# Attention units of 384, 384 and 320 columns, and one token order for all batches, in a polysketch attention and mixture-of-experts kernel

## The chip, the cores and the metric

The kernel runs on one core of a Trainium2 chip. A core has five engines that run their own instruction queues and meet only through semaphores: PE (TensorE, matrix products), DVE (VectorE), ACT (ScalarE), POOL (GpSimd) and SP, which in this kernel issues nearly all DMAs. The metric is the device time of one launch in microseconds; lower is better. The time given is the median of several runs; the profile is one profiled execution.

## The reference, cut to what matters

There are 4 batches, 4 heads, 1088 tokens and head dimension 32; then 4352 tokens of width 128 go through 4 experts with hidden width 1024. Everything is float32.

```
def phi(x):                       # polynomial sketch, 8 x 8 = 64 features
    a = einsum('rd,bhsd->bhsr', S1, x); b = einsum('rd,bhsd->bhsr', S2, x)
    return einsum('bhsi,bhsj->bhsij', a, b).reshape(..., 64)
q_p, k_p = phi(q), phi(k)
kv  = einsum('bhsf,bhsd->bhfd', k_p, v);   z = sum(k_p, axis=s)
x   = (q_p @ kv) / (q_p @ z + 1e-6)        # then (B,H,S,D) -> (B*S, H*D)
p   = domain_probs / (sum(domain_probs) + 1e-9)
out = sum over e of p[:, e] * (relu(x @ w1[e]) @ w2[e])
```

The attention of a batch needs all its keys first (kv and z sum over tokens). After that each token's query row is independent, and so is each token in the experts.

## The kernel before, in words

**Columns.** Tokens are columns of the tile `xT` (128 features x 4352). Inside a batch, column c stands for token (c % 32) * 34 + c // 32 (G = 34): a partition of the loaded `qn` holds 34 consecutive tokens, and a 32x32 vector transpose turns 32 partitions into 32 neighbouring columns. The last batch is the exception in this kernel: its columns are loaded as 30 tokens per partition for the first 960 columns and 4 per partition for the last 128 (lines 95 to 97), so that its last 128 columns are 128 tokens in a row. The loads of the gate probabilities `dp` and `ends` (lines 150 to 158) and the output addresses (lines 860 and 904) follow that order.

**Expert work: chunks and steps.** `CHUNKS` cuts the 4352 columns into 11 chunks (128, 448, six of 512, 320, 256, 128), and `START` gives their first columns: 0, 128, 576, 1088, 1600, 2112, 2624, 3136, 3648, 3968, 4224. A chunk takes 16 steps: 4 experts times 4 pairs of hidden blocks. In a step, `first` makes two halves: each is a product `h` into one of three PSUM banks (pool `ps_h`), a relu on ACT (line 817), and one or two rectify-and-subtract instructions on DVE (line 786) that make the operand combinations for a 7-product scheme. After `first(i)` comes `second(i - 2)`: seven products `o` of half the chunk's width. Products use half the array's columns (64) each; `on_side` hands them to the two halves in turn. After the fourth step of an expert, `gather` copies `o` on ACT and POOL adds the pieces and multiplies by the gate (lines 923 to 943). Chunks 0 and 10 are plain (no 7-product scheme).

**Attention work: pieces.** The attention of batches 1 to 3 and of the rest of batch 0 is a generator, `front`. It is cut into pieces by its `yield`s: 19 pieces for the keys of a batch (three transposes `key_turn`, line 328; three projections on PE; eight products `key_product` on DVE, line 391, whose both inputs are in SBUF; `key_sum` on PE) and 20 pieces for each unit of query columns (transpose, projection, three shuffles, four products `qp` (line 501), then `attend`: PE products, reciprocal, multiplication, a transpose to `y` (line 591), four stores to the DRAM tile `xd` (line 609) and one load into `xT` (line 617)). `UNITS` gives the widths of a batch's units. A unit of up to three 128-column blocks uses one bank in `attend`, a wider one uses two.

**What sets the order.** The queues are written out by this Python program. In each half step, after the relu and the rectify instructions, `work()` adds credit, and for each whole credit it emits the next piece. The credit per step is `rate`, the largest need over all later chunks:

```
rate = CHUNKS[m] / NQ * max([0] + [(needed[c] + (8 if c > 1 else 4) - done[0]) / (START[c] - gone) for c in range(m + 1, NC)])
```

`needed[c]` is the number of pieces after which the columns of chunk c are there; it follows from `UNITS` and `CHUNKS`. The rest of SP's queue (next batch's loads after its predecessor's keys, the gate loads at the sixth step of a chunk, the output stores) is placed by the same program.

Of the kernel before, what the change touches and what calls it, by code (L numbers as in the profile page):

```python
# [16 lines left out]
def _ap(t, p0: int, np_: int, off: int, free):  # L17

    p = list(t.ap)[0]
    return bass.AP(t.tensor, t.offset + p0 * p[0] + off, [[p[0], np_]] + [list(d) for d in free])  # L20
# [3 lines left out]
def kernel(  # L24
# [20 lines left out]

    nc = tc.nc

    P = 128
    HP = 64
    B, H, S, D = q.shape
    E, DM, F = w1.shape
    R = 8
    R2 = 2 * R
    G = S // 32
# [5 lines left out]
    CW = 512  # L63
    GE = 160
    LA = 2
    UNITS = [[P, 448, 512], [512, 320, 256], [448, 512, P], [384, 320, 384]]

    CHUNKS = [P, 448, 512] + [512] * 5 + [320, 256, P]
    NC = len(CHUNKS)
    START = [sum(CHUNKS[:m]) for m in range(NC)]  # L70
    assert all(sum(u) == S for u in UNITS) and sum(CHUNKS) == B * S

# [11 lines left out]
    def psum(pool, tag):  # L84
        return pool.tile([P, 512], F32, tag=tag, name=tag)


    def load_rows(src, b, name, part=slice(0, S)):

        d = kn if name == "kn" else qn  # L90
        if b not in d:
            d[b] = lpool.tile([P, S], F32, tag=name, bufs=2, name=name)
        c, n = part.start, part.stop - part.start
        base = src.offset + b * H * S * D
        if name == "qn" and b == B - 1:
            for c, n, t in ((0, (G - 4) * D, 0), ((G - 4) * D, 4 * D, S - P)):
                nc.sync.dma_start(d[b][:, c : c + n], bass.AP(src.tensor, base + t * D, [[S * D, H], [n, 32], [1, n]]))
        else:
            nc.sync.dma_start(d[b][:, part], bass.AP(src.tensor, base + c, [[G * D, P], [1, n]]))

    def load_v(b):
        t = lpool.tile([P, H * NT * D], F32, tag="vn", name="vn")
# [13 lines left out]
    kn, qn, vn = {}, {}, {}  # L116

    def load_batch(b):
        load_rows(k, b, "kn")
        vn[b] = load_v(b)  # L120
        load_rows(q, b, "qn")
# [7 lines left out]
    def load_w1(e):  # L129
        nc.sync.dma_start(w1_sb[:, e, :], w1[e])  # L130

    def load_w2(e):
        nc.sync.dma_start(w2_sb[:, e], w2[e].rearrange("(f p) d -> p f d", p=P))

    load_rows(k, 0, "kn")
    load_rows(q, 0, "qn", slice(0, P))
    vn[0] = load_v(0)
# [6 lines left out]
    dp = cpool.tile([P, G, E], F32, name="dp")  # L144

    ends = cpool.tile([P, 2, E], F32, name="ends")
    e_sum = cpool.tile([P, 2, 3], F32, name="e_sum")
    load_rows(q, 0, "qn", slice(P, S))
    load_w1(0)
    for p0, n, g0, m, t in ((0, 96, 0, G, 0), (96, 32, 0, G - 4, 3 * S), (96, 32, G - 4, 4, B * S - P)):  # L150
        nc.sync.dma_start(
            _ap(dp, p0, n, g0 * E, [[1, m * E]]),
            bass.AP(domain_probs.tensor, domain_probs.offset + t * E, [[m * E, n], [1, m * E]]),
        )
    for i, t, g in ((0, 0, G), (1, B * S - P, 4)):
        nc.sync.dma_start(
            ends[:, i, :], bass.AP(domain_probs.tensor, domain_probs.offset + t * E, [[g * E, 32], [1, 4 * E]])
        )
    load_w2(0)
    for e in range(1, E):  # L160
# [37 lines left out]
    def on_side(out, weights, moving, **flags):  # L198

        s = turn[0]  # L200
        turn[0] = 1 - s
        nc.tensor.matmul(out(s), weights(s), moving(s), **flags)  # L202
# [97 lines left out]
    def parts(m):  # L300

        c, end, at = START[m], START[m] + CHUNKS[m], 0
        while c < end:
            n = min(end, (c // S + 1) * S) - c
            yield c // S, c % S, n, at
            c, at = c + n, at + n
# [367 lines left out]
    def start():  # L674


        b, n = 0, UNITS[0][0]
        kf = []
# [39 lines left out]

        n1 = UNITS[b][1]
        qT = apool.tile([P, QW], F32, tag="qT2", name="qT2")  # L720
# [14 lines left out]
    def front():  # L735
        for b in range(B):
# [4 lines left out]
            c = 0  # L741
            for n in UNITS[b]:
                if b or c:
# [5 lines left out]
    hid, acc, total = {}, {}, {}  # L749
    NP = FB // 2  # L750

    def plain(m):
        return m in (0, NC - 1)
# [77 lines left out]
    def second(i):  # L831
        m, kq = steps[i]
        n, (e, f) = CHUNKS[m], divmod(kq, NP)
        hd = hid.pop(i)
        if plain(m):

            if f == 0:
                acc[m] = psum(ps_o, f"o{e % 2}")
            for j in range(2):
                for _ in range(2):  # L840
                    on_side(
                        lambda s: acc[m][half[s], 0:DM],
                        lambda s: hd[:, n * j + HP * s : n * j + HP * s + HP],
                        lambda s: w2_sb[:, e, 2 * f + j, :],
                        start=(f == j == 0),
                        stop=(f == NP - 1 and j == 1),
                    )
            if f == NP - 1:
                p_e = ends[:, 1 if m else 0, e : e + 1]
                if e == 0:  # L850
                    total[m] = mpool.tile([P, P], F32, tag="end", name="end")
                    nc.vector.tensor_scalar(
                        out=total[m][:, :], in0=acc[m][:, 0:DM], scalar1=p_e, scalar2=None, op0=ALU.mult
                    )
                else:
                    nc.vector.scalar_tensor_tensor(  # L856
                        out=total[m][:, :], in0=acc[m][:, 0:DM], scalar=p_e, in1=total[m][:, :], op0=ALU.mult, op1=ALU.add
                    )
                if e == E - 1:
                    t, to = (B * S - P, [[DM, P], [1, DM]]) if m else (0, [[G * DM, 32], [1, 4 * DM]])  # L860
                    nc.sync.dma_start(bass.AP(out.tensor, out.offset + t * DM, to), total.pop(m)[:, :])
            return
        if f == 0:
            acc[m, e] = [psum(ps_o, "o0"), psum(ps_o, "o1")]
            begun[:] = [0, 0]
        w = n // 2
        blk = lambda a, j: w2_sb[:, e, 2 * f + j, HP * a : HP * a + HP]
        new = lambda a: w2s[:, e, f, a, :]
        place = lambda a: hd[:, w * a : w * a + w]

        todo = (
            [(blk(0, 0), place(0)), (new(3), place(3)), (blk(0, 1), place(2)), (new(1), place(6))],
            [(new(2), place(5)), (new(0), place(4)), (blk(1, 1), place(7)), (new(1), place(6))],
        )
        at = [0, 0]
        for _ in range(7):
            s = turn[0]
            p = at[s]
            at[s] += 1

            fresh = p >= begun[s]
            begun[s] = max(begun[s], p + 1)
            wt, mv = todo[s][p]
            on_side(
                lambda s: acc[m, e][p // 2][half[s], w * (p % 2) : w * (p % 2) + w],
                lambda s: wt,
                lambda s: mv,
                start=(fresh and p % 2 == 0),
                stop=(f == NP - 1),
                skip_group_check=True,  # L890
            )

    def turn_back(m, src):

        n = CHUNKS[m]
        ob = mpool.tile([P, CW], F32, tag="ob", name="ob")
        nc.vector.transpose(ob[:, 0:n], src)
        for b, c, nn, at in parts(m):
            for a in range(4):
                nc.sync.dma_start(  # L900
                    bass.AP(
                        out.tensor,
                        out.offset + (b * S + c // 32) * DM + 32 * a,
                        [[(G - 4 if b == B - 1 else G) * DM, 32], [DM, nn // 32], [1, 32]],
                    ),
                    _ap(ob, 32 * a, 32, at, [[32, nn // 32], [1, 32]]),
                )
# [54 lines left out]

    needed, columns, count = [0] * NC, UNITS[0][0], 0
    for b in range(B):
        count += 19 if b else 0
        for n in UNITS[b] if b else UNITS[0][1:]:
            count, columns = count + (20 if count else 18), columns + n
# [8 lines left out]
    for i in range(len(steps) + LA):  # L976
        if i < len(steps):
            m, kq = steps[i]
# [34 lines left out]
        if i >= LA:  # L1013
            second(i - LA)
            mm, kk = steps[i - LA]
            if kk % NP == NP - 1 and not plain(mm):
                ending = chain(ending, gather(mm, kk // NP))
            else:
                next(ending, None)
# [29 lines left out]
```

## Time and profile before

| What | Value |
|---|---|
| median of 3 runs | 487.64 us (487.64 to 488.46) |
| the profiled execution: its own time | 487.64 us |
| its span | 485.9 us |
| PE busy | 481.5 us (99%) |
| DVE busy | 320.9 us (66%) |
| ACT busy | 246.8 us (51%) |
| POOL busy | 230.0 us (47%) |
| granted TensorE clock | 1.0 in all slices |
| DMA, q1 | 25.53 MB, 18.9% of 16 engines' span |

Busy PE time counts a product from its modelled start to its end, and products overlap, so 99% says that PE was rarely without a product. The 40 slices of the page show where an engine was busy; the list of waits says for whom an engine stood idle; the chain follows back from the last instruction to whatever released each step.

### The profile page before, as it was taken

Reading aid. Unit: us, or ns where it says so; the run is one execution under the profiler, and the core shown is the slowest. Engines: PE = TensorE matmul, PEld = TensorE weight load, DVE = VectorE, ACT = ScalarE, POOL = GpSimd, SP = SyncE. Lnnn points to the kernel's source line nnn. Section 1 sums busy time; section 2 is a strip of 40 time slices with the busy share of each in tenths; the row PEclk is TensorE's granted clock in tenths of the full one; section 3 lists DMA queues with packets and bytes.
Section 4 is the critical chain, followed back from the end, with each engine's and each line's share of the span. In section 5 each row is a group of like instructions: output and inputs, shape, how many; then the busy total and the mean of one; then the engine's idle time right before and its main releaser. Section 6 shows DMA issues by size and latency. Waiting matters only on the chain.

```text
span 485.9 us, 11377 instructions
## 1 busy us (share of the span) xinstructions
PE 481.5 (99%) x4551; PEld 362.7 (75%) x4551; DVE 320.9 (66%) x759; ACT 246.8 (51%) x496; POOL 230.0 (47%) x270
## 2 busy tenths in 40 slices
PE   8999999999999999999999999999999999999997
PEld 6965666667777777777777777677777777999997
DVE  6859675686766668486776757668684666665642
ACT  4354564445544555355445555445455555566651
POOL 5172654435444455415455444424555445555571
PEclk9999999999999999999999999999999999999999
DMA  7990050211003123031103100021101200120001
GB/s 223 278 299 10 23 150 12 88 20 45 2 9 106 24 69 93 2 89 20 40 1 130 24 12 1 3 86 24 34 0 56 50 1 0 45 55 4 15 1 20
DMA packets 37772, 26.25 MB, mean 54 GB/s; under 512 B 24824, under 2 KB 34520, under 8 KB 37208
## 3 DMA queue, kind: packets, MB, share of 16 engines
q1 hardware_dynamic: 37704, 25.53, 18.9%
q8 instruction: 36, 0.59, 0.5%
q14 instruction: 16, 0.13, 0.1%
q10 hardware_dynamic: 16, 0.00, 0.0%
HBM read 21.28 MB, written 4.24 MB: 53 GB/s over the span
## 4 chain that ended last, share of the span: by engine, by line
PE 97%; DMA 1%; DVE 1%; issue 0%; SPq 0%; ACT 0%; ACTq 0%
PE h L202 50%; PE o L202 41%; PE f L202 3%; PE den L202 2%; DMA kn<-in_k_dram 1%; PE num L202 1%; DVE qp L501 0%; DVE kp L391 0%; DVE kT L328 0%; DVE qT L488 0%; SPq L125 0%; DVE end L856 0%; DVE kvz L414 0%; ACT fs L360 0%; ACT vx L337 0%
## 5 line engine op out<-in xcount | busy, mean ns | idle before, releaser
L202 PE MATMUL h<-xT,w_sb 128*64 128x512 f32 (+5 forms) x1424 | 300.2, 491 | 0.0
L786 DVE SCALAR_TENSOR_TENSOR hid<-h,hid 128x256 f32<-128x256 f32 (+6 forms) x432 | 203.7, 472 | 143.3 <-ACT hid L817 134.9
L817 ACT ACTIVATE hid<-h 128x512 f32<-128x512 f32 (+3 forms) x288 | 158.5, 550 | 192.3 <-PE h L202 146.2
L202 PE MATMUL o<-hid,w2s 128*64 128x256 f32 (+3 forms) x1152 | 224.0, 355 | 0.0
L202 PEld LDWEIGHTS h<-xT,w_sb 128*64 128x64 f32 x1424 | 147.5, 137 | 50.4 <-issue 6.4
L202 PE MATMUL o<-hid,w_sb 128*64 128x256 f32 (+3 forms) x864 | 183.7, 355 | 0.0
L202 PEld LDWEIGHTS o<-hid,w2s 128*64 128x64 f32 x1152 | 132.2, 137 | 28.9
L930 POOL TENSOR_TENSOR ev<-yz,sh 64x256 f32<-64x256 f32 (+3 forms) x72 | 48.7, 676 | 159.9 <-ACT sh L933 157.2
L202 PEld LDWEIGHTS o<-hid,w_sb 128*64 128x64 f32 x864 | 100.5, 137 | 25.2 <-issue 5.8
L918 POOL TENSOR_TENSOR yz<-ev 128x512 f32<-128x512 f32 (+3 forms) x36 | 41.7, 1160 | 60.4 <-ACT ev L921 60.2
L930 POOL TENSOR_TENSOR ct<-ev 128x512 f32<-128x512 f32 (+3 forms) x36 | 42.5, 1182 | 2.8
L930 POOL TENSOR_TENSOR total<-total,ct 128x512 f32<-128x512 f32 (+3 forms) x27 | 31.9, 1181 | 2.1
L930 POOL TENSOR_TENSOR ct<-ct,gate 128x512 f32<-128x512 f32 (+3 forms) x27 | 31.8, 1177 | 2.1
L501 DVE TENSOR_TENSOR qp<-qa,qb 64x512 f32<-64x512 f32 (+5 forms) x44 | 30.1, 685 | 1.0
L920 ACT COPY ev<-o 128x512 f32<-128x512 f32 (+3 forms) x36 | 19.4, 539 | 12.7 <-PE o L202 12.3
L202 PE MATMUL o<-w_sb,hid 128*64 128x128 f32 x256 | 22.3, 273 | 0.0
L921 ACT COPY ev<-o 128x512 f32<-128x512 f32 (+3 forms) x36 | 19.4, 539 | 2.0
L202 PEld LDWEIGHTS o<-w_sb,hid 128*64 128x64 f32 x256 | 18.1, 137 | 1.6 <-issue 0.9
L809 ACT ACTIVATE hid<-h 128x256 f32<-128x256 f32 x23 | 8.4, 384 | 18.3 <-PE h L202 17.9
L391 DVE TENSOR_TENSOR kp<-fs 128x256 f32<-128x256 f32 (+1 forms) x24 | 16.6, 696 | 0.1
L933 ACT COPY sh<-yz 64x256 f32<-64x256 f32 (+3 forms) x36 | 13.7, 380 | 1.7 <-POOL yz L918 0.8
L202 PEld LDWEIGHTS den<-kvx,qp 128*64 128x64 f32 x240 | 12.5, 137 | 2.5 <-issue 0.5
(129 smaller groups left out, 247.5 us busy)
## 6 DMA issues: line engine op xcount, KB each, us to landing
w_sb<-in_moe_w_dram SPq DMA_DIRECT2D x8, 512.0 KB, 5.8
gate<-gates SPq DMA_DIRECT2D x4, 1024.0 KB, 4.7
kn<-in_k_dram SPq DMA_DIRECT2D x4, 544.0 KB, 7.0
vn<-in_v_dram SPq DMA_DIRECT2D x16, 128.0 KB, 3.5
gate<-gates SPq DMA_DIRECT2D x2, 896.0 KB, 6.4
qn<-in_q_dram SPq DMA_DIRECT2D x2, 544.0 KB, 4.0
out_dram<-ob SPq DMA_DIRECT2D x16, 64.0 KB, 2.0
qn<-in_q_dram SPq DMA_DIRECT2D x2, 480.0 KB, 5.0
```

The lines of the kernel that those rows point to most:

```text
L202: nc.tensor.matmul(out(s), weights(s), moving(s), **flags)
L391: eng.tensor_tensor(out=_ap(kps[b], 0, P, 256 * t0 + P * p + 64 * x, [[256, n], [32, 2], [R, 4], [1, R]]), in0=_ap(src, 0, P, off + 4 * x, ...
L501: nc.vector.tensor_tensor(out=qp[p][64 * x : 64 * x + 64, 0:n], in0=qa[64 * p : 64 * p + 64, 0:n], in1=qb[64 * p : 64 * p + 64, 0:n], op=A ...
L786: nc.vector.scalar_tensor_tensor(out=out, in0=src, scalar=0.0, in1=in1, op0=ALU.max, op1=ALU.subtract)
L809: nc.scalar.activation(hd[:, 0 : 2 * n], hp[:, 0 : 2 * n], ACTF.Relu)
L817: nc.scalar.activation(hd[:, n * j : n * j + n], hp[:, 0:n], ACTF.Relu)
L918: add = lambda out, in0, in1, op=ALU.add: nc.gpsimd.tensor_tensor(out=out, in0=in0, in1=in1, op=op)
L920: nc.scalar.copy(_ap(ev, 0, P, 0, [[2 * w, 2], [1, w]]), _ap(a0, 0, P, 0, two))
L921: nc.scalar.copy(_ap(ev, 0, P, w, [[2 * w, 2], [1, w]]), _ap(a1, 0, P, 0, two))
L930: add = lambda out, in0, in1, op=ALU.add: nc.gpsimd.tensor_tensor(out=out, in0=in0, in1=in1, op=op)
L933: nc.scalar.copy(sh[HP:P, 0:w], yz[0:HP, 0, 0:w])
```

## The change

Three things are edited; no instruction's arithmetic changes.

- **Units.** Batches 1 and 2 are cut as 384, 384, 320 columns, where they were 512, 320, 256 and 448, 512, 128. Batches 0 and 3 keep their units. `CHUNKS` stays, so that the ends of units and chunks now fall on other columns, and `needed` becomes 0, 18, 38, 97, 117, 176, 196, 235, 255, 275, 275, where it was 0, 18, 38, 77, 117, 156, 176, 235, 255, 275, 275. With it the rate and the place of nearly every piece from chunk 1 to chunk 6 change.
- **Token order.** The last batch's columns are ordered as the other batches' are. Its `qn` is loaded by one DMA (two before); `dp` by one (three before); `ends[1]` reads with the common stride.
- **Output addresses.** The last batch's stores use the stride of 34 rows as the others do, and the last chunk's 64 KB store goes to 32 runs of 2 KB, where it was one run of 64 KB.

```
-    UNITS = [[P, 448, 512], [512, 320, 256], [448, 512, P], [384, 320, 384]]
+    UNITS = [[P, 448, 512]] + [[384, 384, 320]] * 2 + [[384, 320, 384]]
...
-        base = src.offset + b * H * S * D
-        if name == "qn" and b == B - 1:
-            for c, n, t in ((0, (G - 4) * D, 0), ((G - 4) * D, 4 * D, S - P)):
-                nc.sync.dma_start(d[b][:, c : c + n], bass.AP(src.tensor, base + t * D, [[S * D, H], [n, 32], [1, n]]))
-        else:
-            nc.sync.dma_start(d[b][:, part], bass.AP(src.tensor, base + c, [[G * D, P], [1, n]]))
+        nc.sync.dma_start(d[b][:, part], bass.AP(src.tensor, src.offset + b * H * S * D + c, [[G * D, P], [1, n]]))
...
-    for p0, n, g0, m, t in ((0, 96, 0, G, 0), (96, 32, 0, G - 4, 3 * S), (96, 32, G - 4, 4, B * S - P)):
-        nc.sync.dma_start(
-            _ap(dp, p0, n, g0 * E, [[1, m * E]]),
-            bass.AP(domain_probs.tensor, domain_probs.offset + t * E, [[m * E, n], [1, m * E]]),
-        )
-    for i, t, g in ((0, 0, G), (1, B * S - P, 4)):
+    nc.sync.dma_start(
+        dp.rearrange("p g e -> p (g e)"), bass.AP(domain_probs.tensor, domain_probs.offset, [[G * E, P], [1, G * E]])
+    )
+    for i, t in enumerate((0, (B - 1) * S + G - 4)):
         nc.sync.dma_start(
...
-                    t, to = (B * S - P, [[DM, P], [1, DM]]) if m else (0, [[G * DM, 32], [1, 4 * DM]])
-                    nc.sync.dma_start(bass.AP(out.tensor, out.offset + t * DM, to), total.pop(m)[:, :])
+                    t = (START[m] // S) * S + START[m] % S // 32
+                    nc.sync.dma_start(
+                        bass.AP(out.tensor, out.offset + t * DM, [[G * DM, 32], [1, 4 * DM]]), total.pop(m)[:, :]
+                    )
...
-                        [[(G - 4 if b == B - 1 else G) * DM, 32], [DM, nn // 32], [1, 32]],
+                        [[G * DM, 32], [DM, nn // 32], [1, 32]],
```

More of the change, by code (lines that the diff above doesn't have):

```diff
@@ L149 @@
     load_w1(0)
-    for p0, n, g0, m, t in ((0, 96, 0, G, 0), (96, 32, 0, G - 4, 3 * S), (96, 32, G - 4, 4, B * S - P)):
+    nc.sync.dma_start(
+        dp.rearrange("p g e -> p (g e)"), bass.AP(domain_probs.tensor, domain_probs.offset, [[G * E, P], [1, G * E]])
+    )
+    for i, t in enumerate((0, (B - 1) * S + G - 4)):
         nc.sync.dma_start(
-            _ap(dp, p0, n, g0 * E, [[1, m * E]]),
-            bass.AP(domain_probs.tensor, domain_probs.offset + t * E, [[m * E, n], [1, m * E]]),
-        )
-    for i, t, g in ((0, 0, G), (1, B * S - P, 4)):
-        nc.sync.dma_start(
-            ends[:, i, :], bass.AP(domain_probs.tensor, domain_probs.offset + t * E, [[g * E, 32], [1, 4 * E]])
+            ends[:, i, :], bass.AP(domain_probs.tensor, domain_probs.offset + t * E, [[G * E, 32], [1, 4 * E]])
         )
```

## The prediction

> **What bounds the kernel now.** I read the page first, then PE's own waits, then the vector queue around the key products, then SP's queue.
>
> ```profile
> PE 481.5 (99%) x4551; PEld 362.7 (75%) x4551; DVE 320.9 (66%) x759; ACT 246.8 (51%) x496; POOL 230.0 (47%) x270
> ...
> PEclk9999999999999999999999999999999999999999
> ...
> PE 97%; DMA 1%; DVE 1%; issue 0%; SPq 0%; ACT 0%; ACTq 0%
> ```
>
> PE carries 97% of the chain at the full granted clock. The complete list of what PE waited for is three early waits, 1.4 us together:
>
> ```profile
> PE h L190 <- PEq L1033: 0.8, 1, 0.8
> PE h L202 <- DVE kT L328: 0.4, 1, 0.4
> PE den L202 <- DVE kvz L414: 0.2, 1, 0.2
> ```
>
> So the change can gain almost nothing; it can lose if a new piece order makes PE wait. The danger lies where DVE is tight, in the timelines of DVE and POOL around batch 1's key products:
>
> ```profile
> 67.04 0.60 DVE L391 TENSOR_TENSOR kp<-fs 128x256 f32<-128x256 f32 x1
> 68.37 0.39 DVE L786 SCALAR_TENSOR_TENSOR hid<-h,hid 128x224 f32<-128x224 f32 x1 [0.72 <-ACT hid L817]
> 68.68 0.93 DVE L391 TENSOR_TENSOR kp<-fs 128x256 f32<-128x256 f32 x1
> 69.54 1.04 DVE L786 SCALAR_TENSOR_TENSOR hid<-h,hid 128x448 f32<-128x448 f32 x2
> 70.49 1.23 DVE L391 TENSOR_TENSOR kp<-fs 128x256 f32<-128x256 f32 x1
> 71.64 0.38 DVE L786 SCALAR_TENSOR_TENSOR hid<-h,hid 128x224 f32<-128x224 f32 x1
> 71.94 0.41 DVE L391 TENSOR_TENSOR kp<-fs 128x256 f32<-128x256 f32 x1
> ```
>
> ```profile
> 67.45 1.20 POOL L930 TENSOR_TENSOR total<-total,ct 128x448 f32<-128x448 f32 x1
> 68.61 0.73 POOL L671 TENSOR_TENSOR w2s<-w_sb,w2s 128x256 f32<-128x256 f32 x1
> 70.30 1.14 POOL L918 TENSOR_TENSOR yz<-ev 128x448 f32<-128x448 f32 x1 [0.97 <-ACT ev L921]
> ```
>
> The reader is to see two things. The same product takes 0.41 us alone and 0.93 or 1.23 while a POOL instruction runs. And from 68.37 on DVE has no idle time left: it has become late, and only buffers hide that from PE.
>
> **The change part by part.** The sum is made against the profiled execution: 485.9 us of span and 1.74 around it, 487.64, which is also the median.
>
> *PE's work: 0.* Query columns stay 1088 a batch. Units of 512+320+256 and 448+512+128 need 4+3+2 and 4+4+1 blocks in `attend`, units of 384+384+320 need 3+3+3: nine each way. Keys and experts are untouched.
>
> *DVE's work: 0.* Three wide units lose their second bank: per unit one 0.15 add and one 0.28 multiplication (rows of lines 573 and 582 of the unit at 111.5 to 113.5), 1.3 us in all, not on the chain.
>
> *Fewer load DMAs: 0.* SP spends 5.94 to 7.68 on three `dp` issues and would spend about 0.4 on one, so `ends` and the weights start 1.3 us earlier. POOL waits 1.7 us for `ends`, but PE never for a DMA here. The two `qn` issues at 185.64 (0.65 and 0.55) become one; their reader comes only at 317. No cover goes, and a gain is excluded because PE waits for none of them.
>
> The Trainium skill, page "DMA: Bandwidth & Descriptors", section "Rules for kernel authors", says that many small transfers should be joined and that under 64 KB one pays mostly overhead, which favours this edit. By that rule I would estimate up to 1.3 us of gain and a time of 487.9 instead of my sum; the waits list, in which PE waits for no DMA, says none.
>
> *The last store: +0.05.* After the last product the tail is
>
> ```profile
> 482.90 0.35 DVE L856 SCALAR_TENSOR_TENSOR end<-o,ends,end 128x128 f32<-128x128 f32 x1 [0.89 <-PE o L202]
> 483.28 0.35 SPq L861 DMA_DIRECT2D out_dram<-end  x1
> ```
>
> and 2.6 us to the end. The new pattern is that of chunk 0's store, which had a 0.65 issue and 3.3 to landing beside load traffic. Bounds -0.05 to +0.8; nearer the quiet row, since nothing else moves then.
>
> *The order of the pieces.* Counting the loops' yields, batch 1's keys are pieces 39 to 57, batch 2's 98 to 116, batch 3's 177 to 195. The rate formula gives pieces per step:
>
> | chunk | before | after | binding chunk after |
> |---|---|---|---|
> | 1 (28 columns a step) | 2.06 | (97+8-22)/960*28 = 2.42, 2.6 late in it | 3 |
> | 2 (32) | 2.40 | (97+8-57)/512*32 = 3.00 | 3 |
> | 3 | 2.41 | 2.47 | 5 |
> | 4 | 2.40 | 2.50 | 5 |
> | 5, 6 | 2.41, 2.44 | 1.84, 1.88 | 7 |
>
> From chunk 7 on both are alike (243 pieces done). Six prices follow.
>
> (a) *Batch 1's key products: +1.0 (0 to 3.8).* Steps of 448 columns without attention take 2.65 us (relus at 54.52 and 57.17). DVE's rectifying takes 0.31 + 0.95 of it, start to start in the rows above. The eight products of this batch average 0.71 (0.60, 0.93, 1.23, 0.41, 0.49, 0.48, 0.49, 1.08). Before: 1.26 + 2.1*0.71 = 2.75 a step, 0.1 over, 0.4 late by the end of 3.8 steps. After: 1.26 + 2.6*0.71 = 3.11, 0.46 over, 1.4 late after 3.1 steps, on top of the about 0.65 that a single 1.23 product leaves (rectify due at 70.99, started 71.64). The cover: the bank of a first half is written again by the second half of the next step. Its rectify ends 0.97 after its relu starts (54.52; 55.10 + 0.39) and the bank is wanted at 57.13, 2.61 after it: 1.6 us. Lateness 2.05 against 1.6 gives 0.45; two products in one half step, each behind a 1.14 us POOL instruction, add about 1.2 more at once. I take 1.0, nearer the mean rows. Low end: no product meets POOL (0.45 each: 2.43 a step, nothing late). High end: all eight at 1.23, 6.2 over the bare ones, less 0.7 of room and 1.6 of cover. What waits behind: PE's `h`, and with it everything.
>
> (b) *Batch 2's: +0.4 (0 to 1.5).* They run at 3.0 to 2.47 instead of 2.4. At 3.22 a step and 1.39 of rectifying, 2.47*0.7 gives 3.12 against 3.07: little more. But they follow query pieces at 3.0 a step, so DVE arrives late.
>
> (c) *Batch 3's: -0.2 (-0.3 to 0.3).* In before its products at 299.68 to 304.5 took up to 1.60, and relus that start 3.26 apart are 3.50 apart once:
>
> ```profile
> 301.90 0.60 ACT L817 ACTIVATE hid<-h 128x512 f32<-128x512 f32 x1 [1.78 <-PE h L202]
> ...
> 305.16 0.60 ACT L817 ACTIVATE hid<-h 128x512 f32<-128x512 f32 x1 [0.32 <-PE h L202]
> ...
> 308.66 0.60 ACT L817 ACTIVATE hid<-h 128x512 f32<-128x512 f32 x1 [2.02 <-PE h L202]
> ```
>
> At 1.85 pieces a step that 0.24 should go.
>
> (d) *Batch 1's first projection: +0.15 (0 to 0.5).* It started at 59.55, 0.79 after its transpose (58.06 + 0.70). Transpose and projection are three half steps apart before, two after: up to 1.3 less lead, partly returned because both now stand in second halves. Likewise the query projections of batch 1 (0.41 of lead at 88.20).
>
> (e) *PE's halves: +0.2 (-0.2 to 0.6).* Seven products a step leave the two halves of the array apart after every odd step. The 16 small products at 50.32, in step, took 0.93 to the next `h`; those at 107.56, halves 0.23 apart, 0.99 on one half. About 24 groups of small products (projections, key sums, `attend`) move to other steps, each worth 0 to 0.06; a shift can help or hurt, and I take a little more hurt, since before may hold most of them well placed.
>
> (f) *Columns in time: 0 (0 to 1.5).* Chunk 3's last columns now come at step 45 instead of 42, three steps ahead of their use. From the first relu of step 42 (112.24) to the landing took 9.2:
>
> ```profile
> 115.66 1.77 SPq L609 DMA_DIRECT2D xd<-y  x4
> 118.92 0.34 SPq L617 DMA_DIRECT2D xT<-xd  x1
> ```
>
> with 2.5 more. Steps 45 to 48 leave 132.15 - 122.42 - 0.82 = 8.9, and the piece sits in a first half, about 1.6 sooner: 7.6 needed, 1.3 to spare. On SP it is moved behind chunk 1's output stores, which were issued by 108.2.
>
> Sum: 1.0 + 0.4 - 0.2 + 0.15 + 0.2 + 0.05 = +1.6, 489.2 us.
>
> The Trainium skill, page "SBUF — State Buffer", section "SBUF: two separate sides", says that a DVE instruction with two SBUF inputs and a GpSimd instruction that reads SBUF exclude each other, and the later one waits for the whole of the earlier. Taken for all eight products of batch 1, that would be an estimated 8 * 1.14 = 9.1 of lateness, 6.8 after room and cover, and 494.4 in place of 489.2; the rows above, 0.71 on average, show that most products miss POOL.
>
> **The rivals.** 0.2% (0.98 us) is about what a measurement of this kernel can tell from no change.
>
> 1. *The cover holds (same).* The three banks hid DVE's lateness throughout chunk 1 before. If the products meet POOL no more than before and (a) stays at 0, the rest is 0.6 us: 488.2. For it: 0.45 of stall is all that the averages give. Against it: DVE has no idle left there already at 2.1 pieces. It decides while DVE stays under 1.6 late.
> 2. *Chunk 3's columns come late (slower).* If DVE is 1.3 us later at step 45, `h` waits for `xT`: up to 1.5 more, 490.7. For it: 3.0 pieces a step. Against it: DVE is idle for most of 109 to 119 before.
> 3. *Relief wins (faster).* The lower rate in chunks 5 and 6 takes away PE losses that the list of waits does not show, as the 0.24 at 305. It would need four such places, 4 * 0.24, with (a) and (b) at 0: 486.7. Only one is in the rows.
>
> **How the numbers follow.** Forecast (key products stall PE) 0.60; rival 2 0.07, also slower; rival 1 0.28; rival 3 0.05. That makes slower 0.67, same 0.28, faster 0.05. The range runs from rival 1 with (a), (b), (d) and (e) at 0 (487.64 - 0.2 + 0.05 = 487.5) to the forecast with (b) at its high end (+1.1) and two fifths of what (a) can add (+1.1), 491.4; the likeliest case alone has 488.7 to 491.4.
>
> **What would show it.** Right: between about 62 and 76 us a step of chunk 1 longer than 2.65 with PE waiting for DVE (`hid` or `kp`), a second place near 170, none near 305; PE's busy total unchanged, span up 1 to 3 us. Wrong: no step of chunks 1 to 3 lengthened; or PE waiting for `xT` at the start of chunk 3; or the tail after the last product longer than 3.0.

## The result

| Kernel | median | lowest to highest | runs |
|---|---|---|---|
| before | 487.62 us | 487.39 to 488.46 | 6 |
| after | 489.15 us | 488.65 to 489.53 | 6 |

The changed kernel takes 1.0028 times as long, with a 95% interval of 1.0015 to 1.0041: slower by 0.7 to 2.0 us. The profiled execution of the changed kernel took 488.65 us with a span of 486.9, against 487.64 and 485.9 before: 1.0 more. It is the fastest of its six runs, and its own time understates the median; the last section says where that comes from.

The page of the changed kernel, busy time and clock, and the chain's shares by engine:

```profile
PE 481.2 (99%) x4551; PEld 368.4 (76%) x4551; DVE 320.0 (66%) x753; ACT 246.9 (51%) x496; POOL 230.7 (47%) x270
...
PEclk9999999999999999999999999999999999999999
...
PE 96%; DVE 2%; DMA 1%; issue 0%; ACT 0%; SPq 0%; ACTq 0%
```

PE does the same products in the same busy time (481.2 after 481.5). But DVE has gone from 1% to 2% of the chain: there are stretches in which the end waited for DVE. The complete list of what PE waited for after the change, and one row of the same list for PE's weight loads (a weight load puts the fixed operand of a product into the array; the columns are engine, line, what it waited for: us, times, longest):

```profile
PE h L194 <- DVE kT L320: 1.0, 1, 1.0
PE h L182 <- PEq L1027: 0.8, 1, 0.8
PE h L194 <- DVE hid L778: 0.3, 1, 0.3
PE den L194 <- DVE kvz L406: 0.2, 1, 0.2
```

```profile
PEld h L194 <- DVE hid L778: 1.3, 2, 1.1
```

PE's row with `hid` is new: `h` waited for DVE's rectify instructions. The weight loads ahead of `h` had such a row before too (1.0, 2, 0.7), but its longest wait stood in chunk 6, at 304.92; now it is one of 1.1 in chunk 1. The 1.0 for `kT` lies at 5.64, ahead of all expert work (0.4 at 5.55 before). Where the new wait is, the chain of the changed kernel shows (start us, us, what):

```profile
63.87 0.45 ACT hid L809
...
64.34 0.64 DVE hid L778
...
65.00 0.39 DVE hid L778
65.39 1.20 DVE kp L383 x2
66.59 0.30 DVE hid L778
...
69.00 1.45 DVE kp L383
70.45 0.31 DVE hid L778
...
70.81 0.97 PE h L194 x4
```

From 64 to 71 us, in the last steps of chunk 1, the chain leaves PE and runs through DVE: products of batch 1's keys, the rectify instructions queued behind them, and then at 70.81 the `h` that was waiting for its bank.

**A measure used below.** To see small losses of PE that no list of waits shows, I added up, in program order and by the same formula for every kernel, the time that PE's products need when nothing disturbs them (the four `h` and seven `o` of a step of 512 columns: 3.23 us), and subtracted that from the time at which the relu of each step starts, counted from the first relu of chunk 1. What is left is time that PE lost since then. It is steady: two profiled executions of the changed kernel end with 1.51 and 1.48 us lost.

| us | before | after | after less before |
|---|---|---|---|
| first relu of chunk 1 | 29.75 | 29.57 | -0.18 |
| lost by step 29 (chunk 1) | 0.18 | 0.18 | 0 |
| lost by step 37 (chunk 2) | 0.23 | 1.09 | +0.86 |
| lost by step 80 (chunk 5) | 0.35 | 1.39 | +1.04 |
| lost by step 98 (chunk 6) | 0.45 | 1.51 | +1.06 |
| lost by step 106 (chunk 6) | 0.79 | 1.60 | +0.81 |
| lost by the last step of chunk 9 | 0.70 | 1.51 | +0.81 |
| last product to the end of the span | 3.00 | 3.39 | +0.39 |

The first, the last but one and the last row make the 1.0 us of the spans (-0.18 + 0.81 + 0.39 = 1.02). So three things need a cause: a loss of 0.86 between steps 29 and 37, a gain of 0.25 between steps 98 and 106, and a longer tail. The 0.18 more by step 80 comes up again under (d) and (e).

### The profile page after: what moved, and what is told of

Read it like the earlier page. It is cut to its first block, busy times and chain, and to the rows that moved or that the text cites. A ratio compares the mean times of both kernels' runs of the same rounds, so it can differ in the third digit from the quotient of the medians.

```text
span 486.9 us, 11369 instructions
## 1 busy us (share of the span) xinstructions
PE 481.2 (99%) x4551; PEld 368.4 (76%) x4551; DVE 320.0 (66%) x753; ACT 246.9 (51%) x496; POOL 230.7 (47%) x270
## 4 chain that ended last, share of the span: by engine, by line
PE 96%; DVE 2%; DMA 1%; issue 0%; ACT 0%; SPq 0%; ACTq 0%
PE h L194 49%; PE o L194 40%; PE f L194 3%; PE den L194 2%; DMA kn<-in_k_dram 1%; DVE kp L383 1%; DVE hid L778 1%; PE num L194 0%; DVE qp L493 0%; DVE kT L320 0%; ACT hid L809 0%; DVE qT L480 0%; SPq L119 0%; DVE end L848 0%; DVE kvz L406 0%
## 5 line engine op out<-in xcount | busy, mean ns | idle before, releaser
L493 DVE TENSOR_TENSOR qp<-qa,qb 64x384 f32<-64x384 f32 (+3 forms) x44 | 30.9, 701 | 1.1
L194 PE MATMUL o<-w_sb,hid 128*64 128x128 f32 x256 | 21.1, 273 | 0.0
L194 PEld LDWEIGHTS o<-w_sb,hid 128*64 128x64 f32 x256 | 16.9, 137 | 1.6 <-issue 0.9
L383 DVE TENSOR_TENSOR kp<-fs 128x256 f32<-128x256 f32 (+1 forms) x24 | 15.0, 634 | 0.1
```

What stands on the lines that cost most here:

```text
L383: eng.tensor_tensor(out=_ap(kps[b], 0, P, 256 * t0 + P * p + 64 * x, [[256, n], [32, 2], [R, 4], [1, R]]), in0=_ap(src, 0, P, off + 4 * x, ...
L493: nc.vector.tensor_tensor(out=qp[p][64 * x : 64 * x + 64, 0:n], in0=qa[64 * p : 64 * p + 64, 0:n], in1=qb[64 * p : 64 * p + 64, 0:n], op=A ...
```

## The experiments

The theory, which the expectations call A: the key products of batch 1 now come closer together in chunk 1, they wait for GpSimd's instructions, DVE falls behind, and the rectify instructions behind them release the banks of `h` too late. Against it stood that the token order with its DMAs makes the difference, and that the loss is PE's own, from where its small products stand among the large ones. Each kernel was compared with the kernel before on the same chip; the first four share 33 runs of it (median 488.07), the last four 17 (487.67).

| Kernel | median | ratio to before, 95% interval | PE lost in all | last product to end |
|---|---|---|---|---|
| e1_units | 489.02 | 1.0019 (1.0010 to 1.0029) | 1.51 | 2.99 |
| e2_order | 488.15 | 1.0002 (0.9993 to 1.0011) | 0.40 | 3.36 |
| e3_pool_after | 488.33 | 1.0006 (0.9998 to 1.0015) | 0.75 | 3.38 |
| e4_pool_before | 487.66 | 0.9993 (0.9982 to 1.0003) | 0.72 | 3.00 |
| e5_rate | 489.22 | 1.0028 (1.0016 to 1.0040) | 1.82 | 2.99 |
| e6_again | 489.01 | 1.0028 (1.0017 to 1.0040) | 1.48 | 3.37 |
| e7_late | 491.24 | 1.0078 (1.0063 to 1.0093) | 3.51 | 3.38 |
| e8_margin12 | 488.16 | 1.0004 (0.9995 to 1.0013) | 0.53 | 3.00 |

### One part of the change alone: units, or token order

e1 is the kernel before with one line changed:

```
-    UNITS = [[P, 448, 512], [512, 320, 256], [448, 512, P], [384, 320, 384]]
+    UNITS = [[P, 448, 512]] + [[384, 384, 320]] * 2 + [[384, 320, 384]]
```

> The kernel before with the new UNITS alone; token order, loads and stores as before. Theory A (the key products of batch 1 meet GpSimd and hold up the banks of h): all of the loss in the stream comes from here, 0.8 to 1.1 us slower than before (488.4 to 488.7), with a rectify of chunk 1 in the chain between 63 and 71 us, and a tail after the last product as before (3.0 us). Theory B (the loss comes from the token order, its loads and its last store): no change, 487.6.

e2 has the rest of the change, and keeps the old units: the loads, the output addresses and the last store.

```
-    for p0, n, g0, m, t in ((0, 96, 0, G, 0), (96, 32, 0, G - 4, 3 * S), (96, 32, G - 4, 4, B * S - P)):
...
+    nc.sync.dma_start(
+        dp.rearrange("p g e -> p (g e)"), bass.AP(domain_probs.tensor, domain_probs.offset, [[G * E, P], [1, G * E]])
+    )
...
-                    t, to = (B * S - P, [[DM, P], [1, DM]]) if m else (0, [[G * DM, 32], [1, 4 * DM]])
+                    t = (START[m] // S) * S + START[m] % S // 32
...
-                        [[(G - 4 if b == B - 1 else G) * DM, 32], [DM, nn // 32], [1, 32]],
+                        [[G * DM, 32], [DM, nn // 32], [1, 32]],
```

> The kernel before with the new token order (loads, last store, output strides) and the old UNITS. Theory A: only the tail moves, the last store's issue 0.60 instead of 0.35 and some 0.15 more to the end: 0.2 to 0.4 us slower (487.8 to 488.0), chunk 1 without a wait. Theory B: 1.0 to 1.5 us slower (488.6 to 489.1).

Measured: e1 is slower, 1.0019, and loses the same 1.51 as the changed kernel, 1.03 of it by step 31 in both. e2 is not to be told from before. So all of the loss in PE's stream comes from the units. The token order shows in one place, at the very end: in the five profiled executions with the new last store (after, e2, e3, e6, e7) the tail is 3.36 to 3.39, in the five with the old one (before, e1, e4, e5, e8) 2.99 to 3.00. The rows of the changed kernel after its last product (start us, us, instruction):

```profile
483.52 0.35 DVE L848 SCALAR_TENSOR_TENSOR end<-o,ends,end 128x128 f32<-128x128 f32 x1 [0.89 <-PE o L194]
483.90 0.60 SPq L853 DMA_DIRECT2D out_dram<-end  x1
```

The issue of the store to 32 runs takes 0.60 (0.58 to 0.60 in the five) where the single run of 64 KB took 0.35; that is 0.25 of the 0.37 to 0.39. The remaining 0.12 to 0.14 lies after the issue, and no run here divides it further.

### Without GpSimd's work in chunk 1

In e3, the changed kernel, and in e4, the kernel before, GpSimd combines only 4 of chunk 1's 448 columns; the combination of that chunk's seven products is left out for the rest, so that these columns of the output are not computed. All products, relus, rectify instructions and key products stay, each at its place.

```
+        w = 2 if m == 1 else w
         yz = mpool.tile([P, 2, CW // 2], F32, tag="yz", bufs=1, name="yz")
...
-        n = CHUNKS[m]
-        w = n // 2
+        n = 64 if m == 1 else CHUNKS[m]
+        w = 2 if m == 1 else n // 2
...
+        if m == 1:
...
+            return
```

> The changed kernel with GpSimd's additions and gate multiplications of chunk 1 cut to 2 columns (left out: the combination of chunk 1's seven products, so that 448 columns of the output are not computed). Everything else, the order of pieces too, stays. Theory A: the key products of batch 1 take 0.41 to 0.49 us each but for those beside the last weight sums, PE doesn't wait for a rectify in chunk 1, and the time falls by 0.6 to 0.8 us below the changed kernel, to about 488.4. Rival C (VectorE alone is too slow at 2.6 pieces per step, GpSimd or not): the loss of 0.85 us in steps 26 to 32 stays, 489.1.

> The control: the kernel before with the same work of GpSimd left out in chunk 1 (448 columns of the output not computed). Theory A and rival C alike: no change beyond 0.2 us (487.5), since nothing of chunk 1 reached PE there. If it gets faster by 0.5 us or more, the cut itself gives time elsewhere and e3 must be read against it.

Measured: e3 comes out at 1.0006, where e1, beside the same 33 runs, had 1.0019. It loses 0.75 in all, 0.76 less than the changed kernel, and the difference is there at once: by step 31 it has lost 0.18, as before the change, where the changed kernel has lost 1.03. The kernel before gains nothing from the same edit (0.72 after 0.70).

DVE's timeline of the changed kernel, then GpSimd's:

```profile
65.31 1.28 DVE L383 TENSOR_TENSOR kp<-fs 128x256 f32<-128x256 f32 x2
66.51 0.38 DVE L778 SCALAR_TENSOR_TENSOR hid<-h,hid 128x224 f32<-128x224 f32 x1
66.81 1.06 DVE L383 TENSOR_TENSOR kp<-fs 128x256 f32<-128x256 f32 x1
67.80 1.04 DVE L778 SCALAR_TENSOR_TENSOR hid<-h,hid 128x448 f32<-128x448 f32 x2
...
69.00 1.45 DVE L383 TENSOR_TENSOR kp<-fs 128x320 f32<-128x320 f32 x1
70.37 0.38 DVE L778 SCALAR_TENSOR_TENSOR hid<-h,hid 128x224 f32<-128x224 f32 x1
```

```profile
66.38 1.21 POOL L924 TENSOR_TENSOR ct<-ev 128x448 f32<-128x448 f32 x1
67.67 1.21 POOL L924 TENSOR_TENSOR ct<-ct,gate 128x448 f32<-128x448 f32 x1
68.97 1.14 POOL L924 TENSOR_TENSOR total<-total,ct 128x448 f32<-128x448 f32 x1
```

The same part of DVE's timeline in e3:

```profile
65.80 0.75 DVE L383 TENSOR_TENSOR kp<-fs 128x256 f32<-128x256 f32 x2
66.47 0.38 DVE L778 SCALAR_TENSOR_TENSOR hid<-h,hid 128x224 f32<-128x224 f32 x1
66.77 0.65 DVE L383 TENSOR_TENSOR kp<-fs 128x256 f32<-128x256 f32 x1
67.34 1.04 DVE L778 SCALAR_TENSOR_TENSOR hid<-h,hid 128x448 f32<-128x448 f32 x2
...
68.54 0.49 DVE L383 TENSOR_TENSOR kp<-fs 128x320 f32<-128x320 f32 x1
68.95 0.38 DVE L778 SCALAR_TENSOR_TENSOR hid<-h,hid 128x224 f32<-128x224 f32 x1
```

The product of 320 columns that starts at 69.00, 0.03 after GpSimd's `total`, takes 1.45; in e3, with that instruction cut, it takes 0.49. The rectify behind it starts at 70.37, 2.76 after its relu (67.61); one that nothing holds up starts 0.58 after it (in e3: 71.09 and 71.67). That is 2.2 late. The second half of the next step waits for that bank. The relus of these two second halves in the changed kernel, then in e3:

```profile
68.32 0.54 ACT L809 ACTIVATE hid<-h 128x448 f32<-128x448 f32 x1 [0.16 <-PE h L194]
...
71.82 0.54 ACT L809 ACTIVATE hid<-h 128x448 f32<-128x448 f32 x1 [0.68 <-PE h L194]
```

```profile
68.81 0.55 ACT L809 ACTIVATE hid<-h 128x448 f32<-128x448 f32 x1 [0.16 <-PE h L194]
...
71.80 0.54 ACT L809 ACTIVATE hid<-h 128x448 f32<-128x448 f32 x1 [0.16 <-PE h L194]
```

They are 3.50 apart, and 2.99 in e3, so 0.51 is lost at this half step. The next relu follows 2.30 later, and 1.96 later in e3: another 0.34, with no further wait for DVE. In e3 one half of the array is ahead of the other here and begins its `o` at 71.25, the other at 71.60; in the changed kernel both began again at 70.81 and reach `o` together at 71.61, so that this lead of 0.35 is lost too. Together that is the 0.85. The chain of e3 over the same stretch has no DVE left in it:

```profile
64.41 1.53 PE h L194 x8
65.94 1.32 PE o L194 x13
67.27 1.50 PE h L194 x8
68.77 1.29 PE o L194 x13
```

Theory A holds: products that wait for GpSimd are what makes PE wait. The rival that it is PE's own order of products falls for this loss, since e3 keeps that order. So does rival C, that DVE is too slow at this pace by itself: e3 has the same DVE instructions at the same pace.

The Trainium skill, page "SBUF — State Buffer", section "SBUF: two separate sides", has a DVE instruction with two SBUF inputs and a GpSimd instruction that reads SBUF exclude each other, the later one waiting for the whole of the earlier. The rows agree in the main: 1.45 beside a `total` of 1.14, 0.49 without it; the rest of `total` and a whole product would be 1.11 + 0.49 = 1.60.

### The rate of the pieces alone

e5 is the kernel before, with its old units, and a larger margin for chunk 3 in the rate formula, which puts the first 57 pieces, the keys of batch 1 among them, at the changed kernel's steps. e7 is the changed kernel with a smaller margin: chunk 1 runs at (97 + 4 - 22) / 960 * 28 = 2.30 pieces a step where the changed kernel has 2.42, and the columns of chunk 3 come one step later.

```
-            rate = CHUNKS[m] / NQ * max([0] + [(needed[c] + (8 if c > 1 else 4) - done[0]) / (START[c] - gone) for c in range(m + 1, NC)])
+            rate = CHUNKS[m] / NQ * max([0] + [(needed[c] + (28 if c == 3 else 8 if c > 1 else 4) - done[0]) / (START[c] - gone) for c in range(m + 1, NC)])
```

> The kernel before with its own UNITS and token order, only the margin of chunk 3 raised from 8 to 28 pieces. That gives the first 57 pieces exactly the steps that they have in the changed kernel (2.42 pieces a step in chunk 1), with the old units behind them. Theory A (the pace in chunk 1 brings the key products onto GpSimd's instructions): the loss of 0.85 us in steps 26 to 32 appears whole, in the chain a rectify between 63 and 71 us, and the time is 0.6 to 1.0 us above the kernel before. Rival D (the widths of the units themselves cost it): no loss in chunk 1, no change.

The edit of e7, against the changed kernel:

```
-            rate = CHUNKS[m] / NQ * max([0] + [(needed[c] + (8 if c > 1 else 4) - done[0]) / (START[c] - gone) for c in range(m + 1, NC)])
+            rate = CHUNKS[m] / NQ * max([0] + [(needed[c] + (4 if c == 3 else 8 if c > 1 else 4) - done[0]) / (START[c] - gone) for c in range(m + 1, NC)])
```

> The changed kernel with chunk 3's margin lowered from 8 to 4 pieces: 2.30 instead of 2.42 pieces a step in chunk 1, and chunk 3's last columns one step later (46 instead of 45). Theory A: less loss in chunk 1 (0.85 falls to 0.3 to 0.6), but if the 1.3 us to spare of step (f) was right, the step of 3.2 us is too much and h waits for xT at the start of chunk 3 by 1.5 to 2.5 us; together 1.0 to 2.0 us slower than the changed kernel. If the columns had more to spare than 3.2 us: faster than the changed kernel by 0.3.

Measured: e5 is as slow as the change (1.0028), with the old units and the old token order. It loses 0.18 by step 29 and 1.09 by step 37, the changed kernel's figures to the hundredth, and its product of 320 columns takes 1.45 too. So the width of the units is not the cause in itself; they act through `needed` and the rate. By its median e5 is 1.55 above the kernel before, where 0.6 to 1.0 was expected; its stream accounts for 1.12 of that (1.82 less 0.70), and what it loses after step 37 was not followed up.

In e7, with 2.30 pieces, PE has lost 0.61 by step 37, 0.38 more than the kernel before. That lies between the two other rates, as theory A expected, but it does not come by way of the rectify instructions: no `h` of chunk 1 waits for one. A weight load of `o` stood 0.34 for `w2s`, one of the sums of weights that GpSimd makes, which in e7 came at 70.68, behind GpSimd's `total`, and ended at 71.67:

```profile
71.72 0.20 PEld L194 LDWEIGHTS o<-hid,w2s 128*64 128x64 f32 x4 [0.34 <-POOL w2s L663]
```

No other kernel shows this wait. So of three rates (2.06, 2.30, 2.42) only the highest makes PE wait for a rectify in chunk 1, and the 0.38 of e7 is no measure of theory A; that it fell into the expected 0.3 to 0.6 is luck.

e7 tests the margin of chunk 3's columns as well. SP's load of them and the chain after it, in e7:

```profile
132.09 0.34 SPq L609 DMA_DIRECT2D xT<-xd  x1
```

```profile
131.04 1.68 PE o L194 x14
132.72 1.87 issue
134.59 1.94 PE h L194 x8
```

PE stood for 1.87 and began chunk 3's first `h` 2.50 after the load was issued. The chain calls that "issue", a wait that it cannot attribute; that it is for these columns follows from its place and from the edit. In the changed kernel the same load is issued at 128.21; with the same 2.50 its columns were there at about 130.71, an estimate, and its first `h` started at 132.45: 1.74 to spare. One step later, 3.23, would by that cost about 1.5. It cost 1.87 of standing still, and 2.4 in the measure of losses between steps 44 and 48 (0.53 to 2.90); what the other 0.5 is was not followed up. In all e7 is 2.2 above the changed kernel beside it (e6), where 1.0 to 2.0 was expected.

### The changed kernel again, and a milder margin

e6 is the changed kernel without an edit. e8 is the kernel before with a margin of 12 where it has 8:

```
-            rate = CHUNKS[m] / NQ * max([0] + [(needed[c] + (8 if c > 1 else 4) - done[0]) / (START[c] - gone) for c in range(m + 1, NC)])
+            rate = CHUNKS[m] / NQ * max([0] + [(needed[c] + (12 if c > 1 else 4) - done[0]) / (START[c] - gone) for c in range(m + 1, NC)])
```

> The changed kernel itself beside the others, for differences on one chip. Every theory: 1.0 to 1.6 us above the kernel before.

> The kernel before with the margin of all chunks at 12 instead of 8 pieces: 2.45 instead of 2.40 pieces a step from chunk 2 on, 2.09 instead of 2.06 in chunk 1. It shifts batch 3's key products by a few pieces. If the 0.27 us that the kernel before loses in step 98 to 99 is a chance meeting with GpSimd's instructions, another place of the pieces loses it or not: 0 to 0.3 us faster than before, or as much slower where a new meeting arises. No theory expects more.

Measured: e6 gives the first result again, 1.0028, with every loss within 0.03 of the first execution's. e8 cannot be told from before. Its stream loses 0.53 where the kernel before loses 0.70: it does not have the 0.31 of step 99 (last section) and loses part of that later. No kernel tried beats the kernel before by more than the comparison can show.

## Why the prediction was right, step by step

The forecast was 489.2 with slower as the likeliest sign, and its mechanism was the one that the runs show. The sum was +1.6; the stream and the tail of the trace make 0.81 + 0.39 = 1.2, and the medians differ by 1.5 (0.7 to 2.0 by the interval). That the sum comes so close is in part luck: (b) was 0.4 too high, the last store 0.33 too low, and the working of (a) does not carry its number.

| Step of the sum | predicted | shown |
|---|---|---|
| PE's work; DVE's work; fewer loads | 0 | PE busy 481.2 after 481.5; DVE 320.0 after 320.9; token order and loads alone 1.0002 |
| (a) batch 1's key products | +1.0 | +0.85 at its place, +0.76 at the end (after against e3) |
| (b) batch 2's | +0.4 | 0.0 |
| (c) batch 3's | -0.2 | -0.25, but not shown to come from the rate |
| (d), (e) first projection and halves | +0.35 | about +0.3 |
| (f) columns in time | 0, 1.3 to spare | 0, 1.74 to spare |
| last store | +0.05 | +0.38 |

- **(a) has the right mechanism and place.** The forecast put DVE 2.05 late against a cover of 1.6, on the bank that a first half leaves for the second half of the next step. The rectify at 70.37 is 2.2 late, and the `h` that starts at 70.81 is that second half. The eight products average (0.41 + 1.28 + 1.06 + 1.45 + 0.71 + 0.88) / 8 = 0.72, where 0.71 was taken. One row was read wrongly: "steps of 448 columns without attention take 2.65" is every other step, since steps alternate between 2.67 and 2.99 (e3: relus at 66.14, 68.81, 71.80) and average 2.83. With 2.83 the accumulated lateness is (3.11 - 2.83) * 3.1 = 0.9 and not 1.4; with the 0.65 of a single long product that is 1.55, within the cover. The average would then have given no loss. What goes with the loss is the order of the collisions: 1.28 for two, 1.06 and 1.45, one after the other. e7, whose long products do not follow each other so, has no late rectify. The forecast's other figure for (a), 494.4 if all eight products met GpSimd, leaves out the remaining 0.6 of its own sum; with it that is 495.0.
- **(b) was mis-sized.** Batch 2's products at 161 to 173 us do meet GpSimd, but no step is longer for it. Rows of the changed kernel, the longest product, the rectify it delays, and the two relus of first halves around that:

```profile
167.61 1.31 DVE L383 TENSOR_TENSOR kp<-fs 128x320 f32<-128x320 f32 x1
168.84 1.14 DVE L778 SCALAR_TENSOR_TENSOR hid<-h,hid 128x512 f32<-128x512 f32 x2
```

```profile
168.76 0.60 ACT L809 ACTIVATE hid<-h 128x512 f32<-128x512 f32 x1 [0.32 <-PE h L194]
...
171.95 0.60 ACT L809 ACTIVATE hid<-h 128x512 f32<-128x512 f32 x1 [1.78 <-PE h L194]
```

  The relus are 3.19 apart, an undisturbed step. The step that failed is "DVE arrives late": it had idle time of 0.90 just before 166.12.
- **(c)** went as said in size: PE lost 0.34 between steps 98 and 106 before, and 0.09 after. But e2, with the old units and batch 3's products still there, loses only 0.03 in that place, and e5 and e8, with the old units too, do not have the loss either. So the lower rate is not shown to have brought the gain; the rows are in the last section, and the right size is luck.
- **(d) and (e)** cannot be told apart. With GpSimd out of the way, e3 has lost as much as the kernel before at step 37 (0.23) and 0.28 more at step 80; it ends 0.05 above it, since (c) comes off. Batch 1's first projection does start right behind its transpose now (the weight load waits 0.53 for `kT`), and starts at 54.76, about 0.1 after one half of the array was free.
- **(f)** held, with 1.74 to spare for 1.3.
- **The last store was mis-sized.** Two rows were at hand: 0.35 for the issue to one run of 64 KB, and 0.65 for the issue with this very pattern in chunk 0. The forecast took the first, "nearer the quiet row, since nothing else moves then", and put the 0.65 down to the load traffic around it. In the quiet it takes 0.60. That a tail over 3.0 would speak against the forecast was on its own list, and this term it did refute.

**The rivals.** That the cover holds fell by a small margin: at 2.30 pieces a step (e7) it still holds, at 2.42 it does not. Chunk 3's columns were in time; delayed on purpose by one step they cost 491.24, where the rival had 490.7. A loss did go away at one place and no other, and e2 shows that it can go without the change.

The Trainium skill, page "DMA: Bandwidth & Descriptors", section "Rules for kernel authors", would have small transfers joined. Here three fewer loads brought nothing that can be seen (e2, with them: 1.0002, 0.9993 to 1.0011; first relu of chunk 1 at 29.93 after 29.75), PE waited for none of them before, and the scattered store that came with them cost 0.38 in the tail.

## What to carry to other kernels

When background work is fed in by a rate, ask which later chunk binds that rate and whether the new one lets contended instructions follow each other without a gap; here their mean hardly moved (0.71 and 0.72), and a few long ones in a row went with the loss. Look at the other engine in the contention as well: in e7 it was GpSimd's own late result that PE waited for. Compare that run of lateness with the time until the buffer behind it is wanted again, with a step length averaged over a full period of the schedule. And price a store at the end of a kernel by the row of the same access pattern, wherever that row is.

## What was not expected of the hardware

**A tie of 0.01 us decides 0.3 us.** The kernel before and e2 issue the same instructions here in the same order. GpSimd's `total` and a key product of 320 columns start within 0.01 us of each other, `total` first both times. Kernel before, DVE's and GpSimd's timelines:

```profile
302.92 1.60 DVE L391 TENSOR_TENSOR kp<-fs 128x320 f32<-128x320 f32 x1
```

```profile
302.91 1.27 POOL L930 TENSOR_TENSOR total<-total,ct 128x512 f32<-128x512 f32 x1
```

The same two instructions in e2:

```profile
303.10 0.49 DVE L383 TENSOR_TENSOR kp<-fs 128x320 f32<-128x320 f32 x1
```

```profile
303.09 1.63 POOL L924 TENSOR_TENSOR total<-total,ct 128x512 f32<-128x512 f32 x1
```

In the first DVE lost the tie and took 1.60; in the second GpSimd did and took 1.63 instead of 1.27. Only in the first does a weight load of `h` then wait long for a rectify:

```profile
304.92 0.20 PEld L202 LDWEIGHTS h<-xT,w_sb 128*64 128x64 f32 x4 [0.72 <-DVE hid L786]
```

The relu of step 99 starts 3.50 after that of step 98 in the one and 3.19 in the other; over steps 98 to 106 PE lost 0.34 and 0.03. In e4, with the same instructions here, DVE lost the tie again (1.61), and the same weight load waited 0.74. What decides the tie the rows do not say. So a forecast by rows of one execution cannot hold a tie for certain: it is a term with two values.

**Where the spread between runs lies.** In the ten profiled executions the first relu of chunk 1 starts between 29.57 (the changed kernel's first profile) and 30.78 us (e5), while the losses after it repeat within 0.03 for the same kernel. Part of it is a wait for the first expert weights, here in e5:

```profile
PE h L202 <- DMA w_sb<-in_moe_w_dram: 1.2, 1, 1.2
```

e6 shows the same wait with 0.4, the changed kernel's first profile none at all. The later start accounts for the 0.3 us in span between two executions of the changed kernel (486.9 and 487.2), and it fits the first profile's place at the low end of its runs, of which no other has a profile. What decides when these weights land was not tried.
